# An attention and mixture-of-experts kernel on one core: exponentials and last sums in PSUM, scaling on ScalarE, kept blocks on SP's queue, shared PSUM banks

## The chip, the cores and the metric

The kernel runs on one core of a Trainium2 chip. The metric is the device time of one execution in microseconds: the median of several runs, and beside it one profiled execution, from which all views come. The engines are TensorE (PE in the profile; PEld is its weight load), VectorE (DVE), ScalarE (ACT), GpSimd (POOL) and SyncE (SP, which only issues transfers). PSUM, which TensorE writes, has eight banks of 512 fp32 values per partition.

## The reference

Attention over 4 batches, 8 heads, 768 positions and 64 channels, with a local window of 96 positions, 8 global positions and a linear distance bias for each head; then four experts of two products each, weighted by `domain_probs`.

```python
scores = scale * q @ k^T + bias            # masked to the window and the global positions
a = exp(scores - max); a = a / (a.sum(-1) + 1e-9)
x = (a @ v) as [3072, 512]
p = domain_probs / (domain_probs.sum(-1) + 1e-9)
for e in range(4):
    out += p[:, e:e+1] * (relu(x @ w1[e]) @ w2[e])
```

## The kernel before

Every matrix of the large products is split into two fp32r parts, a rounded one and the rest, and each product is three matmuls. The attention of batch 0 runs alone at the start (`early=True`, plain fp32 operands); the attention of batch b+1 then runs beside the experts of batch b; the last batch's experts run alone.

**Attention.** Heads go in pairs, a pair has six tiles of 128 positions. `flow` (line 472) is one step of a software pipeline of four stages: the scores of a new tile, the softmax of the tiles of the two steps before, the transposition (`turn`, line 434) of the next older one, and, once three tiles are collected, the products with v (`weigh`, line 446). In `softmax` (line 402), for each of the two heads, VectorE adds the bias to the scores, writes `pb` in SBUF and takes the row's extreme; ScalarE takes the exponential in `pb` and sums it into `zsum`; for the older tile VectorE adds 1e-9, takes the reciprocal and multiplies `pb`. The score tile `ps` holds both heads, 256 columns each. `prepare` (line 493) makes the operands of a pair in six steps: transposes through PSUM tiles `pt`, the split of q into `st_q` and of k into `kd`, and four transfers that copy a half of `st_q` to `qd`, of which there is one buffer. `prepare_early` (line 356) does it for the start; there VectorE writes the second half of the partitions of `early_q` and ScalarE the first, both from one `pt`.

**Experts.** A unit is a quarter of one expert's hidden columns: sixteen units a batch. `first` (line 730) makes the hidden part h by seven block products in place of eight (a Strassen scheme), each of six matmuls with 384 columns into a PSUM tile `pm`. VectorE adds each `pm` to earlier sums in SBUF (`p1`, `u`, `vv`, `c22`); ScalarE's ReLU makes the rounded part of h; the rest of h is put on the list `late` and made by VectorE after the next addition. `second` (line 769) makes six groups of six matmuls with 512 columns, and VectorE adds each to `acc`. `blocks` (line 587) makes the seven operand blocks (`xB`, `xT`) from the next batch's x, on VectorE, ScalarE and GpSimd, during the last products of a batch.

**Weights.** In batch 0 `load_w1` and `load_w2` (lines 648 and 688) load and split each unit's weights on ScalarE and GpSimd, step by step beside the products, and `keep` (line 639) writes the split block to DRAM by GpSimd's queue at once. Later batches fetch it by SP's queue, which also carries q, k, v, the raw weights and the copies to `qd`.

**PSUM banks.** At the start: three `ps`, four `pt`, one `px`. Later: three `pm`, two `ps`, two `pt`, one `px`.

**Order.** To the seventh step of batch 0's experts each engine's instructions stay in program order (`Ordered.on`). After that a list scheduler orders them, with program order as its priority, and tracks dependences and buffers.

Of the kernel before, what the change touches and what calls it, by code (L numbers as in the profile page):

```python
# [9 lines left out]
F32 = mybir.dt.float32  # L10
# [8 lines left out]
P = 128  # L19
# [6 lines left out]
def f32(ap):  # L26
    return ap.bitcast(F32)
# [158 lines left out]
def attn_moe_kernel(ctx: ExitStack, tc, q, k, v, n_global, n_local, domain_probs, w1, w2, out):  # L186
# [88 lines left out]
    class Pools:  # L275


        def __init__(self, stack, name, st, kd, qd, nat, natv, pb, ps, pt):
            def sbuf(part, bufs):
                return stack.enter_context(tc.tile_pool(name=f"{name}_{part}", bufs=bufs))  # L280

            def psum(part, bufs):
                return stack.enter_context(tc.tile_pool(name=f"{name}_{part}", bufs=bufs, space=PSUM))

            self.st, self.natv = sbuf("st", st), sbuf("natv", natv)
            self.kd, self.qd, self.nat, self.vg = sbuf("kd", kd), sbuf("qd", qd), sbuf("nat", nat), sbuf("vg", kd)
            self.pb, self.pT, self.small = sbuf("pb", pb), sbuf("pT", 4), sbuf("small", pb)
            self.ps, self.pt, self.px = psum("ps", ps), psum("pt", pt), psum("px", 1)
# [33 lines left out]

    def prepare_q(A, nat, hf, got):

        tp = transpose_half(A, nat, hf)
        st = A.st.tile([P, 2, HALF], F32R, name="st_q")
        ac.activation(st[:, 0, :], tp[:, :HALF], AF.Copy, scale=-SCALE)
        yield
        ve.scalar_tensor_tensor(
            st[:, 1, :], tp[:, :HALF], -SCALE, f32(st[:, 0, :]), op0=ALU.mult, op1=ALU.subtract  # L330
        )
        qd = got[("q", hf)] = A.qd.tile([P, 2, 2, HALF], F32R, name="qd")
        for j in range(2):
            for n in range(2):
                sy.dma_start(f32(qd[n * D : (n + 1) * D, j]), f32(st[j * D : (j + 1) * D]))

    def prepare_k(A, nat, hf, got):
# [11 lines left out]
        yield  # L349
# [52 lines left out]
    def softmax(A, new, old):  # L402
# [12 lines left out]
        for j in range(2):  # L415
            if new:
                ve.tensor_tensor_reduce(
                    new["pb"][:, j, pcol], ps[:, j, cols], nbias[:, 2 * pr + j, bcol],
                    1.0, 3.0e38, ALU.add, ALU.min, nmax[:, j : j + 1],
                )  # L420
                ac.activation(
                    new["pb"][:, j, pcol], new["pb"][:, j, pcol], AF.Exp, bias=nmax[:, j : j + 1], scale=-1.0,
                    accum_out=new["zsum"][:, j : j + 1],
                )
            if old:
                if j == 0:
                    ve.tensor_scalar_add(zsum, zsum, 1e-9)
                else:
                    ve.reciprocal(zsum, zsum)
        if old:  # L430
            for j in range(2):
                ve.tensor_scalar_mul(pb[:, j, old["pcol"]], pb[:, j, old["pcol"]], zsum[:, j : j + 1])
# [13 lines left out]
    def weigh(A, three, x):  # L446

        px = A.px.tile([P, 512], F32, name="px")
# [17 lines left out]
    def attention(b, A, early=False):  # L466
# [5 lines left out]
        def flow(new=None):  # L472

            one, two, three, four = tiles
            if new:
                new["ps"] = scores(A, new["t"], gots[new["pr"]], early)
            if three and not early:
                turn(A, three)
            softmax(A, one, two)
            if three and early:  # L480
                turn(A, three)
            if four:
                turned.append(four)
                if len(turned) == TPH:
                    weigh(A, turned, x)
                    turned.clear()
            tiles[:] = [new, one, two, three]
# [5 lines left out]
        def prepare(nat, got):  # L493

            got["v"] = nat
            q0, q1 = (prepare_q(A, nat["q"], hf, got) for hf in range(2))
            k0, k1 = (prepare_k(A, nat["k"], hf, got) for hf in range(2))
            next(q0)
            yield 1
            next(q0, None)  # L500
            next(k0)
            yield 1
            next(k0, None)
            yield 1
            next(k1)
            yield 1
            nat["vg"] = windows(A, nat["v"])
            next(k1, None)
            next(q1)
            yield 1  # L510
            next(q1, None)
# [125 lines left out]
    kept = {}  # L637

    def keep(key, dst):
        kept[key] = dp.tile(list(dst.shape), F32R, name="kept_{}_{}_{}".format(*key))  # L640
        po.dma_start(f32(kept[key]), f32(dst))
# [6 lines left out]
    def load_w1(i, wait=0, lead=5, hold=2):  # L648
# [37 lines left out]
        keep((e, g, 1), dst)  # L686

    def load_w2(i, lead=7):
# [17 lines left out]
        keep((e, g, 2), dst)  # L706
# [23 lines left out]
    def first(i):  # L730
# [13 lines left out]
        p1, u, vv, c22 = (up.tile([P, HALF], F32, name=n) for n in ("p1", "u", "vv", "c22"))  # L744
# [8 lines left out]
        add(c22, pm, vv)  # L753
        add(u, pm, u)
        relu(1, 1, c22)
        yield
        add(p1, product(i, "A12", "B21"), p1)
        relu(0, 0, p1)
        yield
        add(vv, product(i, "S4", "B22"), vv)  # L760
        relu(0, 1, vv)
        yield
        add(u, product(i, "A22", "T4"), u)
        relu(1, 0, u)
# [4 lines left out]
    def second(i):  # L769

        b, e, g = units[i]
        w2s, h = wts[(i, 2)], hs[i]
# [32 lines left out]
    with ExitStack() as start_stack:  # L805
        A = Pools(start_stack, "start", st=1, kd=2, qd=1, nat=2, natv=3, pb=4, ps=3, pt=4)
# [14 lines left out]
    ps_mm = main.enter_context(tc.tile_pool(name="ps_mm", bufs=3, space=PSUM))  # L821
    A = Pools(main, "att", st=1, kd=1, qd=1, nat=1, natv=1, pb=2, ps=2, pt=2)
# [79 lines left out]
```

## Time and profile before

| | us |
|---|---|
| median of 3 runs | 1236.85 (1235.83 to 1238.42) |
| the profiled execution | 1238.11 |
| its span | 1236.3 |
| mean granted TensorE clock | 0.989 |

The span runs from the first to the last instruction. Stages: attention alone to about 80 us; experts of batch 0 with the attention of batch 1 to about 380; two more such batches to about 675 and 970; the last batch alone to 1230. A wait is put down to what ended last before the waiting instruction began. The busy time of an engine leaves out waits; of overlapping matmuls the union is counted.

### The profile page before, as it was taken

What the parts mean: (1) busy time and instruction counts of PE and PEld (TensorE: products, weight loads), DVE (VectorE), ACT (ScalarE), POOL (GpSimd) and SP (SyncE); (2) the same over time, 40 slices, a digit from 0 to 9 for tenths busy, and PEclk for the clock granted to TensorE, in tenths of its full rate; (3) what the DMA queues carried; (4) which work ended last, traced back from release to release, by engine and by line L of the source; (5) the groups of instructions that cost most, each with busy time, mean ns of one, the idle gap of its engine ahead of it and who ended that gap; (6) DMA issues with size and microseconds to landing.
All of it is one profiled execution on the core that took longest, in us unless ns stands there. A gap on an engine that the chain in (4) does not pass through costs nothing.

```text
span 1236.3 us, 18009 instructions
## 1 busy us (share of the span) xinstructions
PE 1184.1 (96%) x6624; PEld 1055.6 (85%) x6624; DVE 922.9 (75%) x2018; ACT 429.7 (35%) x1044; POOL 241.2 (20%) x258
## 2 busy tenths in 40 slices
PE   6779999999999999999999999999999999999998
PEld 4558898888888898898987898899898899999996
DVE  6878989877868777777767776867776866666665
ACT  4764454545442333333323233333332211111110
POOL 5576657466541000000002000000000100000000
PEclk9989999999999999999999999999999999999999
DMA  6557868786856666576655765757554555555532
GB/s 160 156 158 249 286 212 278 239 282 230 295 183 210 228 197 207 189 228 194 222 169 176 263 195 193 232 166 248 191 170 179 181 213 187 188 187 187 187 128 88
DMA packets 122704, 251.39 MB, mean 203 GB/s; under 512 B 83184, under 2 KB 91376, under 8 KB 106224
## 3 DMA queue, kind: packets, MB, share of 16 engines
q1 hardware_dynamic: 114256, 197.73, 50.5%
q0 software_dynamic: 4608, 46.14, 9.2%
q10 hardware_dynamic: 3744, 6.30, 1.4%
q8 instruction: 54, 0.88, 0.3%
q14 instruction: 42, 0.34, 0.1%
HBM read 174.11 MB, written 52.43 MB: 183 GB/s over the span
## 4 chain that ended last, share of the span: by engine, by line
PE 81%; DVE 9%; DMA 5%; ACT 2%; issue 1%; SPq 1%; POOL 1%; ACTq 0%; DVEq 0%; POOLq 0%
PE pm L42 71%; DMA qd<-st_q 5%; PE pt L42 4%; PE px L42 3%; PE ps L42 3%; DVE pb L42 3%; DVE h L42 1%; SPq L42 1%; DVE x L42 1%; ACT pb L42 1%; DVE zsum L42 1%; DVE u L42 1%; DVE xT L42 0%; DVE acc L42 0%; DVE vv L42 0%
## 5 line engine op out<-in xcount | busy, mean ns | idle before, releaser
L42 PE MATMUL pm<-w2s,h 128*128 128x512 f32 x2304 | 558.5, 396 | 9.5 <-DVE acc L42 9.1
L42 PEld LDWEIGHTS pm<-w2s,h 128*128 128x128 f32 x2304 | 429.1, 189 | 101.3 <-DVE acc L42 12.3
L42 DVE SCALAR_TENSOR_TENSOR acc<-pm,prob,acc 128x512 f32<-128x512 f32 x360 | 267.4, 748 | 120.9 <-PE pm L42 119.1
L42 PE MATMUL pm<-xT,w1s 128*128 128x384 f32 x1536 | 298.4, 339 | 4.9 <-ACT xT L42 3.0
L42 PEld LDWEIGHTS pm<-xT,w1s 128*128 128x128 f32 x1536 | 268.3, 189 | 8.2 <-ACT xT L42 3.4
L42 PE MATMUL pm<-xB,w1s 128*128 128x384 f32 x1152 | 229.1, 340 | 2.2 <-DVE vv L42 1.3
L42 PEld LDWEIGHTS pm<-xB,w1s 128*128 128x128 f32 x1152 | 202.5, 189 | 8.1 <-DVE vv L42 1.6
L42 ACT ACTIVATE pb<-pb,nmax 128x256 f32<-128x256 f32 (+1 forms) x192 | 93.1, 486 | 121.3 <-DVE nmax L42 114.2
L42 POOL COPY vg<-v 32x768 f32<-32x768 f32 x16 | 13.3, 829 | 525.7 <-DMA v<-in_v_dram 515.2
L42 ACT COPY p<-pm 128x384 f32<-128x384 f32 x64 | 30.6, 477 | 214.0 <-PE pm L42 213.9
L42 DVE TENSOR_SCALAR pb<-pb,zsum 128x256 f32<-128x256 f32 (+1 forms) x192 | 84.9, 474 | 2.8
L42 DVE TENSOR_TENSOR u<-pm,p 128x384 f32<-128x384 f32 x64 | 35.6, 556 | 61.1 <-PE pm L42 57.5
L42 DVE CUSTOM_DVE_ANT_0 pb<-ps,nbias 128x256 f32<-128x256 f32 (+1 forms) x192 | 71.9, 395 | 10.9 <-PE ps L42 7.1
L42 ACT ACTIVATE h<-c 128x384 fp32r<-128x384 f32 x64 | 33.6, 525 | 131.8 <-DVE c L42 131.8
L42 ACT COPY pT<-pt 128x512 f32<-128x512 f32 (+1 forms) x96 | 52.2, 544 | 76.0 <-PE pt L42 75.7
L42 DVE TENSOR_TENSOR u<-pm,u 128x384 f32<-128x384 f32 x128 | 70.5, 551 | 3.3 <-PE pm L42 2.6
L42 PE MATMUL pt<-ident,pb 128*128 128x128 f32 x352 | 57.2, 280 | 13.6 <-DVE pb L42 13.0
L42 PEld LDWEIGHTS pt<-ident,pb 128*128 128x128 f32 x352 | 43.3, 143 | 22.6 <-DVE pb L42 6.3
L42 PE MATMUL ps<-kd,qd 128*128 128x256 f32 x288 | 48.6, 283 | 6.0 <-DMA qd<-st_q 6.0
L42 PEld LDWEIGHTS ps<-kd,qd 128*128 128x128 f32 x288 | 44.5, 188 | 11.2 <-issue 7.2
L42 DVE TENSOR_TENSOR c<-pm,vv 128x384 f32<-128x384 f32 x64 | 35.6, 556 | 22.4 <-PE pm L42 21.7
L42 DVE TENSOR_TENSOR vv<-pm,u 128x384 f32<-128x384 f32 x64 | 35.6, 556 | 21.7 <-PE pm L42 21.0
(89 smaller groups left out, 1117.6 us busy)
## 6 DMA issues: line engine op xcount, KB each, us to landing
w1s<-kept SPq DMA_DIRECT2D x48, 1792.0 KB, 7.4
w2s<-kept SPq DMA_DIRECT2D x48, 1024.0 KB, 5.0
kept<-w1s POOLq DMA_DIRECT2D x16, 1792.0 KB, 6.6
qd<-st_q SPq DMA_DIRECT2D x96, 192.0 KB, 6.2
raw<-in_moe_w_dram SPq DMA_DIRECT2D x32, 512.0 KB, 4.4
kept<-w2s POOLq DMA_DIRECT2D x16, 1024.0 KB, 6.6
v<-in_v_dram SPq DMA_DIRECT2D x16, 384.0 KB, 4.2
out_dram<-acc ACTq DMA_DIRECT2D x24, 256.0 KB, 3.0
```

The source lines that it names most:

```text
L42: ins = fn(*args, **kwargs)
```

## The change

- At the start (`A.early`) the biased scores and the exponentials are written over the scores in `ps`; VectorE scales from there into `pb`. `ps` gets four banks, `pt` three.
- In the other batches the exponentials stay in `pb`, and both the addition of 1e-9 and the scaling move to ScalarE.
- `px` has no bank of its own there: it takes a buffer of `pt`. `pm` gets four banks.
- `weigh` comes before the transposition and the softmax in a step.
- The last four sums of `first` are written over `pm`; ReLU and the rest read `pm`. The tile `c22` goes.
- `prepare` makes q's and k's halves whole, in the order q0, k0, q1, k1.
- The kept blocks are written by SP's queue, when the unit's `first` or `second` begins.

```diff
-            self.ps, self.pt, self.px = psum("ps", ps), psum("pt", pt), psum("px", 1)
+            self.ps, self.pt = psum("ps", ps), psum("pt", pt)
+            self.px, self.pxname = (psum("px", px), "px") if px else (self.pt, "pt")
...
+                e = new.setdefault("exp", {})[j] = ps[:, j, cols] if A.early else new["pb"][:, j, pcol]
                 ve.tensor_tensor_reduce(
-                    new["pb"][:, j, pcol], ps[:, j, cols], nbias[:, 2 * pr + j, bcol],
-                    1.0, 3.0e38, ALU.add, ALU.min, nmax[:, j : j + 1],
+                    e, ps[:, j, cols], nbias[:, 2 * pr + j, bcol], 1.0, 3.0e38, ALU.add, ALU.min, nmax[:, j : j + 1]
                 )
                 ac.activation(
-                    new["pb"][:, j, pcol], new["pb"][:, j, pcol], AF.Exp, bias=nmax[:, j : j + 1], scale=-1.0,
-                    accum_out=new["zsum"][:, j : j + 1],
+                    e, e, AF.Exp, bias=nmax[:, j : j + 1], scale=-1.0, accum_out=new["zsum"][:, j : j + 1]
                 )
             if old:
-                if j == 0:
+                if j == 1:
+                    ve.reciprocal(zsum, zsum)
+                elif A.early:
                     ve.tensor_scalar_add(zsum, zsum, 1e-9)
                 else:
-                    ve.reciprocal(zsum, zsum)
+                    ac.activation(zsum, zsum, AF.Copy, bias=1e-9)
         if old:
             for j in range(2):
-                ve.tensor_scalar_mul(pb[:, j, old["pcol"]], pb[:, j, old["pcol"]], zsum[:, j : j + 1])
+                if A.early:
+                    ve.tensor_scalar_mul(pb[:, j, old["pcol"]], old["exp"][j], zsum[:, j : j + 1])
+                else:
+                    ac.activation(pb[:, j, old["pcol"]], old["exp"][j], AF.Copy, scale=zsum[:, j : j + 1])
...
                 new["ps"] = scores(A, new["t"], gots[new["pr"]], early)
+            if four:
+                turned.append(four)
+                if len(turned) == TPH:
+                    weigh(A, turned, x)
+                    turned.clear()
             if three and not early:
                 turn(A, three)
             softmax(A, one, two)
             if three and early:
                 turn(A, three)
-            if four:
-                turned.append(four)
-                if len(turned) == TPH:
-                    weigh(A, turned, x)
-                    turned.clear()
...
-            q0, q1 = (prepare_q(A, nat["q"], hf, got) for hf in range(2))
-            k0, k1 = (prepare_k(A, nat["k"], hf, got) for hf in range(2))
-            next(q0)
-            yield 1
-            next(q0, None)
-            next(k0)
...
+            prepare_q(A, nat["q"], 0, got)
+            yield 1
+            prepare_k(A, nat["k"], 0, got)
+            yield 1
+            prepare_q(A, nat["q"], 1, got)
+            yield 1
+            prepare_k(A, nat["k"], 1, got)
             yield 1
             nat["vg"] = windows(A, nat["v"])
-            next(k1, None)
-            next(q1)
-            yield 1
-            next(q1, None)
+            yield 1
             yield 1
...
-    def keep(key, dst):
-        kept[key] = dp.tile(list(dst.shape), F32R, name="kept_{}_{}_{}".format(*key))
-        po.dma_start(f32(kept[key]), f32(dst))
+    def keep(i, n):
+
+        if (i, n) in waiting:
+            key, dst = waiting.pop((i, n))
+            kept[key] = dp.tile(list(dst.shape), F32R, name="kept_{}_{}_{}".format(*key))
+            sy.dma_start(f32(kept[key]), f32(dst))
...
-        keep((e, g, 1), dst)
+        waiting[(i, 1)] = (e, g, 1), dst
...
+        def last(pm, other):
+
+            add(pm[:, :HALF], pm, other)
+            return pm[:, :HALF]
+
+        p1, u, vv = (up.tile([P, HALF], F32, name=n) for n in ("p1", "u", "vv"))
+        keep(i, 1)
...
         pm = product(i, "S3", "T3")
-        add(c22, pm, vv)
         add(u, pm, u)
-        relu(1, 1, c22)
-        yield
-        add(p1, product(i, "A12", "B21"), p1)
-        relu(0, 0, p1)
-        yield
-        add(vv, product(i, "S4", "B22"), vv)
-        relu(0, 1, vv)
-        yield
-        add(u, product(i, "A22", "T4"), u)
-        relu(1, 0, u)
+        relu(1, 1, last(pm, vv))
+        yield
+        relu(0, 0, last(product(i, "A12", "B21"), p1))
+        yield
+        relu(0, 1, last(product(i, "S4", "B22"), vv))
+        yield
+        relu(1, 0, last(product(i, "A22", "T4"), u))
...
+        keep(i, 2)
         w2s, h = wts[(i, 2)], hs[i]
...
-        A = Pools(start_stack, "start", st=1, kd=2, qd=1, nat=2, natv=3, pb=4, ps=3, pt=4)
+        A = Pools(start_stack, "start", st=1, kd=2, qd=1, nat=2, natv=3, pb=4, ps=4, pt=3, px=1, early=True)
...
-    ps_mm = main.enter_context(tc.tile_pool(name="ps_mm", bufs=3, space=PSUM))
-    A = Pools(main, "att", st=1, kd=1, qd=1, nat=1, natv=1, pb=2, ps=2, pt=2)
+    ps_mm = main.enter_context(tc.tile_pool(name="ps_mm", bufs=4, space=PSUM))
+    A = Pools(main, "att", st=1, kd=1, qd=1, nat=1, natv=1, pb=2, ps=2, pt=2, px=0, early=False)
```

More of the change, by code (lines that the diff above doesn't have):

```diff
@@ L275, in attn_moe_kernel, with __init__ @@
     class Pools:
-        def __init__(self, stack, name, st, kd, qd, nat, natv, pb, ps, pt):
+        def __init__(self, stack, name, st, kd, qd, nat, natv, pb, ps, pt, px, early):
+            self.early = early
             def sbuf(part, bufs):
@@ L446, in weigh @@
     def weigh(A, three, x):
-        px = A.px.tile([P, 512], F32, name="px")
+        px = A.px.tile([P, 512], F32, name=A.pxname)
         for i, tile_ in enumerate(three):
@@ L495, in prepare @@
             got["v"] = nat
-            q0, q1 = (prepare_q(A, nat["q"], hf, got) for hf in range(2))
-            k0, k1 = (prepare_k(A, nat["k"], hf, got) for hf in range(2))
-            next(q0)
+            prepare_q(A, nat["q"], 0, got)
             yield 1
-            next(q0, None)
-            next(k0)
+            prepare_k(A, nat["k"], 0, got)
             yield 1
-            next(k0, None)
+            prepare_q(A, nat["q"], 1, got)
             yield 1
-            next(k1)
+            prepare_k(A, nat["k"], 1, got)
             yield 1
             nat["vg"] = windows(A, nat["v"])
-            next(k1, None)
-            next(q1)
             yield 1
-            next(q1, None)
             yield 1
@@ L636, in attn_moe_kernel @@
     dp = main.enter_context(tc.tile_pool(name="dp", bufs=1, space=bass.MemoryType.DRAM))
-    kept = {}
-    def keep(key, dst):
-        kept[key] = dp.tile(list(dst.shape), F32R, name="kept_{}_{}_{}".format(*key))
-        po.dma_start(f32(kept[key]), f32(dst))
+    kept, waiting = {}, {}
+    def keep(i, n):
[3 more added lines that the diff above has]
+            sy.dma_start(f32(kept[key]), f32(dst))
     def fetch(name, key, shape, view):
@@ L705, in load_w2 @@
             yield 1
-        keep((e, g, 2), dst)
+        waiting[(i, 2)] = (e, g, 2), dst
     hs = {}
@@ L742, in add @@
             work_late()
-        p1, u, vv, c22 = (up.tile([P, HALF], F32, name=n) for n in ("p1", "u", "vv", "c22"))
+        def last(pm, other):
[3 more added lines that the diff above has]
+        keep(i, 1)
         pm = product(i, "A11", "B11")
```

## The prediction

> **What bounds the kernel now.** I read the page's totals first, then the waits of TensorE, then the chain of waits, and after that each stage by itself.
>
> ```profile
> PE 1184.1 (96%) x6624; PEld 1055.6 (85%) x6624; DVE 922.9 (75%) x2018; ACT 429.7 (35%) x1044; POOL 241.2 (20%) x258
> ```
>
> TensorE is busy for 96%, but its matmuls overlap, so this figure hides short stops. The pace is read better from the chain of waits (start, length, what): groups that run without a stop near the end of the third batch, then the last batch, which has no attention beside it.
>
> ```profile
> 940.70 3.13 PE pm L42 x18
> 944.26 5.48 PE pm L42 x24
> 967.97 262.21 PE pm L42 x1302
> ```
>
> A 384-column matmul takes 3.13/18 = 0.174 us, a 512-column one 5.48/24 = 0.228. A batch has 672 and 576 of them: 117 + 131 = 248 us. The last batch runs at that pace, so the diff can win only where TensorE stops. The waits (total, times, longest), first of the whole run, then of 100 to 340 us, then of 660 to 680:
>
> ```profile
> PE pt L42 <- DVE pb L42: 13.0, 16, 1.9
> PE pm L42 <- DVE acc L42: 9.1, 6, 2.0
> PE ps L42 <- DMA qd<-st_q: 6.0, 8, 2.0
> ...
> PE pm L42 <- DVE acc L42: 3.1, 3, 1.3
> PE pm L42 <- DVE vv L42: 1.3, 1, 1.3
> PE pm L42 <- DVE u L42: 0.8, 1, 0.8
> PE pm L42 <- DVE p L42: 0.3, 1, 0.3
> ...
> PE pm L42 <- DVE acc L42: 2.0, 1, 2.0
> ```
>
> There are three places to change: the start, where attention runs alone (its wait is for pb); VectorE's lags in the first mixed batch (3.1 + 1.3 + 0.8 + 0.3 = 5.5 us); and the three batch boundaries, 2.0 us each. The windows show what else a boundary costs, and what the start is bound by (columns: PE, PEld, DVE, ACT, POOL busy, granted clock, DMA share, GB/s):
>
> ```profile
> 11.30:76.60 65.30, 50.36 (x368) 39.53 (x368) 57.13 (x214) 46.70 (x146) 33.26 (x36) 0.96 0.48 138
> ...
> 378.70:382.10 3.40, 3.37 (x8) 2.70 (x9) 2.56 (x4) 0.83 (x1) 0.00 (x0) 0.50 0.02 8
> 675.60:679.00 3.40, 3.40 (x10) 2.62 (x9) 3.40 (x5) 1.66 (x2) 0.00 (x0) 0.50 0.00 0
> 969.20:972.50 3.30, 3.30 (x9) 2.55 (x8) 3.29 (x5) 1.62 (x2) 0.00 (x0) 0.50 0.00 0
> ```
>
> After each boundary's stop the granted clock is 0.50 for 3.4 us, which costs 1.7 us more: 3 x (2.0 + 1.7) = 11.1 us in all. In the start VectorE is busy 57.1 of 65.3 us, and its only long wait there is 6.3 us for `early_q`: the start is VectorE's.
>
> **The change, part by part.**
>
> *Start: exponentials in PSUM.* The groups of VectorE between 11.3 and 76.6 us (24 tiles):
>
> ```profile
> L42 DVE TENSOR_SCALAR pb<-pb,zsum 128x256 f32<-128x256 f32 x39 | 18.9, 526 | 0.7
> L42 DVE CUSTOM_DVE_ANT_0 pb<-ps,nbias 128x256 f32<-128x256 f32 x40 | 16.6, 415 | 0.1
> L42 DVE TENSOR_SCALAR zsum<-zsum 128x2 f32<-128x2 f32 x24 | 6.5, 271 | 0.0
> L42 DVE TENSOR_SCALAR pb<-pb,zsum 128x128 f32<-128x128 f32 x8 | 4.6, 610 | 0.1
> ...
> L42 DVE COPY early_k<-pt 128x384 f32<-128x384 f32 x7 | 3.9, 551 | 0.7 <-PE pt L42 0.7
> ...
> L42 DVE CUSTOM_DVE_ANT_0 pb<-ps,nbias 128x128 f32<-128x128 f32 x8 | 2.2, 285 | 1.4 <-PE ps L42 1.4
> ```
>
> The scaling reads and writes SBUF and is stretched, to 610 ns for half the columns; the add that reads PSUM is not (415 and 285 ns). From PSUM I give the scaling those prices: 39 x (526 - 415) + 8 x (610 - 285) = 6.9 us less. What VectorE pays to write PSUM, no row shows; I take zero more, and for the range the 0.11 us by which the two prices above differ, 48 x 0.11 = 5.3 us to either side.
>
> Against this stands a wait that the diff does not name. Both heads' exponentials now lie in one tile `ps`, 2 x 256 x 4 bytes, one bank. The timeline shows how the program treats a bank that two engines use (start, length, engine):
>
> ```profile
> 41.49 0.48 ACT L42 ACTIVATE early_q<-pt 64x384 f32<-64x384 f32 x1
> 42.01 0.56 DVE L42 TENSOR_SCALAR early_q<-pt 64x384 f32<-64x384 f32 x1 [1.39 <-ACT early_q L42]
> 42.82 0.08 DVE L42 DVE_READ_ACCUMULATOR2_ANT nmax<- 128x1 f32 x1
> 43.00 0.40 ACT L42 ACTIVATE pb<-pb,nmax 128x128 f32<-128x128 f32 x1 [0.26 <-DVE nmax L42]
> 46.20 0.51 ACT L42 ACTIVATE pb<-pb,nmax 128x256 f32<-128x256 f32 x1 [0.74 <-DVE zsum L42]
> 46.61 0.18 ACT L42 ACTIVATION_READ_ACCUMULATOR pb<-pb,nmax 128x1 f32 x1
> ```
>
> The two halves of `early_q` share nothing but the bank of `pt` that they read, on different partitions, yet VectorE starts 0.04 us after ScalarE ends. So the second head's add will wait for the first head's exponential. The hop to ScalarE is 0.10 us (42.90 to 43.00), exponential and accumulator 0.59 (46.20 to 46.79), the hop back 0.04: 0.73 us, in which VectorE, in program order, has only the sum of `zsum` (0.27) to do. It idles 0.46 x 24 = 11.0 us.
>
> The Trainium skill, "PSUM — Partial Sum Buffer", section "PSUM bank collisions raise a hardware error", says that two engines may be in one bank at once only in different quadrants of 32 partitions. By it the halves of `early_q` could have run together, which this trace contradicts with its 0.04 us; for exponentials on all 128 partitions rule and row both give the wait, and the sum by the rule alone is the same.
>
> ScalarE's queue adds to the wait, since a first exponential now holds VectorE up wherever ScalarE is late.
>
> ```profile
> L42 ACT COPY pT<-pt 128x512 f32<-128x512 f32 x80 | 46.4, 580 | 76.0 <-PE pt L42 75.7
> L42 ACT CAST w1s<-sums 128x512 fp32r<-128x512 f32 x32 | 18.6, 615 | 1.3 <-POOL sums L42 1.3
> L42 ACT COPY x<-px 128x384 f32<-128x384 f32 x32 | 15.3, 479 | 39.8 <-PE px L42 39.7
> ```
>
> Between the end of a tile's second exponential and the next first one VectorE leaves ScalarE about 0.8 us (two scalings 0.83, next add 0.42, a hop 0.10, less the 0.59 of the exponential). The copy to `pT` (0.58) fits; with a weight cast (0.615) behind it, ScalarE is 0.4 us late, less where VectorE copies keys: 12 casts x 0.3 = 3.5 us. Start: 11.0 - 6.9 + 3.5 = **+7.6 us** (+2 to +13).
>
> *Products: four banks, last sums in place.* One boundary, in the timeline:
>
> ```profile
> 371.49 0.79 DVE L42 SCALAR_TENSOR_TENSOR h<-c,h 128x384 fp32r<-128x384 f32 x1
> 372.67 1.87 DVE L42 SCALAR_TENSOR_TENSOR h<-p,h 128x384 fp32r<-128x384 f32 x1
> 374.93 2.14 DVE L42 TENSOR_TENSOR xT<-x,xT 128x768 fp32r<-128x768 f32 x1
> 377.94 2.06 DVE L42 SCALAR_TENSOR_TENSOR acc<-pm,prob,acc 128x512 f32<-128x512 f32 x3
> 378.73 3.64 PE L42 MATMUL pm<-w2s,h 128*128 128x512 f32 x8 [2.01 <-DVE acc L42]
> ```
>
> TensorE has filled its three banks and waits for the first `acc`, behind stretched work with two SBUF inputs. With its source in PSUM I price `h<-p` at 0.55 (the key copy above, 551 ns, reads PSUM at that width): 1.3 us earlier. A fourth bank gives TensorE six more matmuls, 6 x 0.228 = 1.4 us. Together this exceeds the stop of 2.0 us; but four of the seven sums now keep their bank through ReLU (about the 0.48 of the x copy) and the rest (0.55), so I leave 0.5 us a boundary, without the half clock: 3 x (3.7 - 0.5) = **-9.6 us** (0 to -11.1). The same bank and the lighter VectorE should take 4.5 of the 5.5 us of lags in the first mixed batch: **-4.5** (0 to -5.5). For the other batches nothing is left to win.
>
> *Scaling on ScalarE in the mixed batches.* The rows of 97 to 357 us:
>
> ```profile
> L42 DVE TENSOR_SCALAR pb<-pb,zsum 128x256 f32<-128x256 f32 x40 | 28.2, 731 | 0.5
> L42 DVE TENSOR_SCALAR zsum<-zsum 128x2 f32<-128x2 f32 x24 | 10.7, 444 | 2.7 <-ACT pb L42 2.7
> ```
>
> VectorE loses about 39 us of work in that batch, ScalarE gains 48 x 0.5 + 24 x 0.2 = 29 us. ScalarE is busy 35% overall, so this lies beside TensorE's work, and its gain is already in the lags above. What it can cost is a ReLU or a `pT` copy behind a scaling (0.5 us), now that ReLU holds a bank. The products with v lose their own bank: 8 a batch wait at worst for one `pT` copy (0.58), 14 us in three batches; no transposition waits for its bank now, so I take **+1** for both.
>
> *Kept blocks on SP's queue, and the preparation's order.* The DMA issues (KB each, us to landing):
>
> ```profile
> kept<-w1s POOLq DMA_DIRECT2D x16, 1792.0 KB, 6.6
> qd<-st_q SPq DMA_DIRECT2D x96, 192.0 KB, 6.2
> ```
>
> GpSimd is spared 32 issues, on no path. On SP, 32 big writes (w2's too) now stand among the loads and the `qd` copies in the first mixed batch; SP waits there only for splits that the products need anyway. The second half of q is prepared earlier, but `qd` has one buffer, so its copies still cannot leave before the scores of tile 2: the 6.0 us of waits for `qd` stay. The copies of 4 second halves have no slack; with a w1 or w2 block ahead 8 times in 10, by half of 6.6 us, 4 x 0.8 x 3.3 = 10.6 us is the upper end, zero the lower. Total traffic is unchanged, and a copy ahead of a block gains, so I take **+2.5**.
>
> Sum: 7.6 - 9.6 - 4.5 + 1 + 2.5 = -3.0 us. The profiled execution took 1238.1 us (span 1236.3, 1.8 around it), 1.3 over the median, so 1235.1 there and 1233.9 against the median: **1234 us**.
>
> **The rivals.**
>
> 1. *Slower, by the start.* The diff puts the products with v, and their copy `x`, ahead of the exponentials in program order. Every third tile the first exponential then waits for 24 matmuls (the chain has 1.46 us for 24) and a copy of 0.48; less 0.4 us of slack that is 1.5 x 8 = 12 us more, 1246. It decides as soon as the start loses 10.6 us instead of 7.6. Against it: TensorE is idle for 15 of the 65 us and may be done early.
> 2. *The fourth bank is eaten up.* If ReLU and rest hold the banks as long as the fourth one lasts, the boundaries still stop for 2.0 us and drop to half clock: 1243.5. For it: ReLU shares ScalarE with the casts of the next batch's blocks there; against it: VectorE is 1.3 us earlier in any case.
> 3. *The add does not wait for the exponential.* Then the start wins 6.9 us, less 2 for a ScalarE that becomes nearly as full: 1233.9 - 7.6 - 4.9 = 1221.5. Against it stands the `early_q` row.
> 4. *Copies of q behind the kept blocks.* With the upper end of 10.6 us, 1242. The Trainium skill, "DMA: Bandwidth & Descriptors", section "Queues, rings and completion order", says that a DMA engine alternates between queue rows packet by packet but takes one row's ring in order; by that rule the move makes this rival likelier. No run here shows it yet.
>
> **How the numbers follow.** Forecast 55%, its own range 1229 to 1239; rivals 12, 10, 15 and 8%. A difference under 0.2% (2.5 us) cannot be told from no change here. Of the forecast's 55, some 32 lie below 1234.4, 15 within 2.5 us of 1236.85 and 8 above; with rival 3 faster has 47%, with rivals 1, 2 and 4 slower has 38%, and 15% is left for the same. The range 1222 to 1245 takes in most of rivals 2 and 4, half of 3 and part of 1.
>
> **What would show it.** The start: the first product begins some 7 us later, and VectorE's waits between 11 and 85 us list a new one for ScalarE's `ps`, about 0.5 us x 24, while its scaling takes about 415 ns. Boundaries: no wait of 2.0 us for `acc`, and a clock of 1.00 after them. Mixed batches: TensorE's waits for `acc`, `vv`, `u` and `p` under 1 us in all. If the wait for `ps` is missing, rival 3 holds; if the windows at the boundaries still show 0.50, rival 2; if TensorE's wait for `qd` passes 10 us, rival 4. A last batch longer than 262 us would mean that the banks do not suffice even without attention, which I have not priced.

## The result and the profile after

| | before | after |
|---|---|---|
| median of 4 runs, us | 1236.34 (1234.34 to 1238.42) | 1221.84 (1221.52 to 1223.60) |
| ratio | 1 | 0.9885 (95%: 0.9869 to 0.9901) |
| span of the profiled execution, us | 1236.3 | 1221.8 |
| mean granted clock | 0.989 | 0.994 |

The kernel is 1.15% faster: 14.2 us at the time of before. The forecast was 1234, which is 0.24% less than before. By the ratio the prediction's before of 1236.85 would become 1222.6 us: at the lowest edge of the range of 1222 to 1245, and below the 1229 to 1239 that the forecast had as its own. So the sign was right and the size was not.

The page's totals of the changed kernel, to be set against the same line of before:

```profile
PE 1176.3 (96%) x6624; PEld 1049.2 (86%) x6624; DVE 835.0 (68%) x1802; ACT 492.9 (40%) x1260; POOL 213.2 (17%) x226
```

VectorE lost 88 us of work, 922.9 to 835.0, and ScalarE gained 63. The waits of TensorE over the whole run (total, times, longest):

```profile
PE pm L42 <- DVE h L42: 3.2, 5, 1.1
...
PE ps L42 <- DMA qd<-st_q: 1.9, 3, 1.1
```

The 9.1 us for `acc` are gone, and of the 6.0 us for `qd` 1.9 are left. Four stretches make up the difference; they are read from one profiled execution of each kernel.

**The start is longer.** The first large product, in the timeline of before (start, length, engine, operation):

```profile
79.83 0.79 PE L42 MATMUL pm<-xB,w1s 128*128 128x384 f32 x3
```

and in the changed kernel:

```profile
92.26 0.79 PE L42 MATMUL pm<-xB,w1s 128*128 128x384 f32 x3
```

It begins 12.4 us later. VectorE's waits from 11.3 to 89.0 us of the changed kernel show why:

```profile
DVE ps L42 <- ACT ps L42: 17.7, 21, 1.9
```

VectorE now waits 17.7 us for ScalarE's exponentials in `ps`. One tile in the timeline:

```profile
44.97 0.45 ACT L42 ACTIVATE ps<-ps,nmax 128x256 f32<-128x256 f32 x1 [1.18 <-DVE nmax L42]
45.34 0.19 ACT L42 ACTIVATION_READ_ACCUMULATOR ps<-ps,nmax 128x1 f32 x1
45.56 0.43 DVE L42 CUSTOM_DVE_ANT_0 ps<-ps,nbias 128x256 f32<-128x256 f32 x1 [0.55 <-ACT ps L42]
```

The second head's add (45.56) starts 0.03 us after ScalarE has read its accumulator for the first head (45.34 + 0.19), although the two heads use different columns: they share the bank.

**The handoff is shorter.** The handoff is the stretch behind the first product, in which the operand blocks are finished beside the products. Here are its large products, in windows of TensorE with the tile `pm` alone (length, busy, matmuls, granted clock, DMA share, GB/s), before:

```profile
79.83:96.93 17.10, 12.40 (x43) 0.70 0.96 303
79.83:119.83 40.00, 31.78 (x132) 0.87 0.78 263
```

and after:

```profile
92.26:109.36 17.10, 15.80 (x78) 1.00 0.95 322
92.26:132.26 40.00, 35.35 (x168) 1.00 0.80 265
```

Before, 43 matmuls in 17.1 us at a clock of 0.70; after, 78 at 1.00. In 40 us the changed kernel is 36 matmuls ahead; at its pace of 40/168 = 0.24 us, 8.6 of the 12.4 us are won back. About 5 of these are the clock: before was granted 0.50 in the window from 85.2 to 95.2 us, behind its first product, the changed kernel in that from 84.7 to 91.4, ahead of it. What sets these stretches is not shown. No step of the forecast holds this.

**The boundaries don't stop.** Where before stood still for 2.0 us and then ran at half clock, the windows after show (PE, PEld, DVE, ACT, POOL, clock):

```profile
373.80:382.00 8.20, 8.20 (x38) 6.68 (x37) 8.20 (x11) 1.98 (x3) 1.43 (x1) 1.00 0.46 188
662.00:670.00 8.00, 8.00 (x36) 6.28 (x35) 8.00 (x9) 1.69 (x3) 1.66 (x1) 1.00 0.49 203
952.00:960.00 8.00, 8.00 (x37) 6.61 (x36) 7.65 (x12) 2.22 (x4) 2.28 (x2) 1.00 0.59 220
```

The chain of waits ends in one piece now, which begins in the last group ahead of the boundary:

```profile
951.21 264.67 PE pm L42 x1320
```

Three boundaries at 3.7 us are 11.1 us. Of these, 3 x 1.7 = 5.1 us are the half clock, and it does not follow from the stops alone: kept_only below stops for 2.0 us at the same three boundaries and keeps a clock of 1.00.

**The mixed batches and the last one.** The last batch keeps its pace: 262.21/1302 and 264.67/1320 are both 0.201 us a matmul. 12.4 - 8.6 - 11.1 = -7.3 us; the other 6.9 us must lie inside the mixed batches. From 100 to 340 us TensorE's waits are now

```profile
PE pm L42 <- DVE h L42: 2.5, 3, 1.1
```

where before had 5.5 us for `acc`, `vv`, `u` and `p`. Part of both lies in the 40 us that are counted above (before 1.3 us for `vv` and 1.3 for `acc`, after 1.1 for h), so 2.8 us against 1.4 are left here. The wait for `qd` is 4.1 us shorter in the whole run. That makes 1.4 + 4.1 = 5.5 of the 6.9 us; where the other 1.4 come from is not shown.

### The profile page after: what moved, and what is told of

It is laid out like the page before. It is cut to its first block, busy times and chain, and to the rows that moved or that the text cites. A ratio compares the mean times of both kernels' runs of the same rounds, so it can differ in the third digit from the quotient of the medians.

```text
span 1221.8 us, 18005 instructions
## 1 busy us (share of the span) xinstructions
PE 1176.3 (96%) x6624; PEld 1049.2 (86%) x6624; DVE 835.0 (68%) x1802; ACT 492.9 (40%) x1260; POOL 213.2 (17%) x226
## 4 chain that ended last, share of the span: by engine, by line
PE 83%; DMA 5%; ACT 4%; DVE 4%; POOL 2%; issue 2%; SPq 0%; ACTq 0%; POOLq 0%; DVEq 0%
PE pm L42 74%; PE pt L42 6%; PE ps L42 3%; DMA qd<-st_q 3%; DMA raw<-in_moe_w_dram 2%; ACT ps L42 2%; DVE ps L42 1%; POOL sums L42 1%; ACT pT L42 1%; POOL w2s L42 1%; POOL w1s L42 1%; SPq L42 0%; PE px L42 0%; DVE pb L42 0%; DVE early_q L42 0%
## 5 line engine op out<-in xcount | busy, mean ns | idle before, releaser
L42 PE MATMUL pm<-w2s,h 128*128 128x512 f32 x2304 | 551.5, 393 | 3.2 <-DVE h L42 3.2
L42 ACT ACTIVATE h<-pm 128x384 fp32r<-128x384 f32 x256 | 124.7, 491 | 177.1 <-DVE pm L42 173.8
L42 DVE SCALAR_TENSOR_TENSOR h<-pm,h 128x384 fp32r<-128x384 f32 x256 | 140.7, 552 | 12.3 <-ACT h L42 8.6
L42 ACT ACTIVATE pb<-pb,nmax 128x256 f32<-128x256 f32 (+1 forms) x144 | 69.9, 487 | 90.4 <-DVE nmax L42 89.8
L42 DVE TENSOR_TENSOR pm<-pm,vv 128x384 f32<-128x384 f32 x128 | 71.6, 560 | 1.4 <-PE pm L42 1.3
L42 ACT ACTIVATE pb<-pb,zsum 128x256 f32<-128x256 f32 (+1 forms) x144 | 63.2, 485 | 18.6 <-DVE zsum L42 18.6
L42 DVE CUSTOM_DVE_ANT_0 pb<-ps,nbias 128x256 f32<-128x256 f32 (+1 forms) x144 | 52.6, 396 | 7.5 <-PE ps L42 3.9
L42 DVE TENSOR_TENSOR u<-pm,u 128x384 f32<-128x384 f32 x64 | 35.6, 557 | 24.1 <-PE pm L42 23.1
L42 POOL TENSOR_TENSOR w2s<-raw,w2s 128x512 fp32r<-128x512 f32 x32 | 40.9, 1293 | 56.2 <-ACT w2s L42 56.2
```

The source lines that it names most:

```text
L42: ins = fn(*args, **kwargs)
```

## The experiments

The kernel before took 1236.0, 1233.7 and 1233.0 us beside the three groups of runs below, so ratios are compared, each to before on its own chip; 0.001 is 1.24 us. The changed kernel stands at 0.9885. It was not run again beside these groups, and the kernel before moved by 3 us between them, so a small difference to the changed kernel has a doubtful size: dve_scale and sums_sbuf are 6.4 and 7.2 us above it by the ratios, 3.8 and 4.1 by the times as they stand. An edit also lets the scheduler order everything behind it anew, and part of a difference may come from that.

| run | us | ratio (95%) |
|---|---|---|
| start_sbuf | 1213.16 | 0.9825 (0.9797 to 0.9852) |
| weigh_late | 1219.23 | 0.9878 (0.9850 to 0.9907) |
| head1_psum | 1206.61 | 0.9775 (0.9748 to 0.9803) |
| kept_pool | 1229.18 | 0.9948 (0.9928 to 0.9968) |
| three_banks | 1247.97 | 1.0122 (1.0105 to 1.0138) |
| sums_sbuf | 1225.95 | 0.9943 (0.9926 to 0.9960) |
| dve_scale | 1225.59 | 0.9937 (0.9921 to 0.9954) |
| head1_weigh_late | 1210.56 | 0.9821 (0.9805 to 0.9837) |
| banks_only | 1221.84 | 0.9925 (0.9897 to 0.9952) |
| kept_only | 1235.40 | 1.0019 (1.0004 to 1.0033) |
| kept_sp_now | 1237.77 | 1.0042 (1.0023 to 1.0060) |
| q_dve_first | 1202.17 | 0.9749 (0.9725 to 0.9773) |

### The start

**start_sbuf**: the changed kernel with the exponentials of the start in SBUF again.

```diff
-e = new.setdefault("exp", {})[j] = ps[:, j, cols] if A.early else new["pb"][:, j, pcol]
+e = new.setdefault("exp", {})[j] = new["pb"][:, j, pcol]
```

> The changed kernel, but at the start the biased scores and exponentials lie in pb (SBUF) as before; banks, order of weigh and all else as changed. In the changed kernel the first product begins at 92.3 us, before at 79.8. Theory (the second head's add waits for the first head's exponential, because both lie in one bank): VectorE's wait for ScalarE's ps (13.9 us) goes, the scaling is stretched again to some 530 ns, and the first product begins at 78 to 83 us; the total falls by most of that, to about 1211 us (1208 to 1216). Rival (weigh's copy x ahead of the exponentials is what lengthens the start): the first product stays past 88 us and the total within 4 us of 1221.8.

Its first large product in the timeline:

```profile
78.84 0.79 PE L42 MATMUL pm<-xB,w1s 128*128 128x384 f32 x3
```

VectorE's scaling in its start (groups from 11.3 to 76.6 us: busy, mean ns, idle before):

```profile
L42 DVE TENSOR_SCALAR pb<-pb,zsum 128x256 f32<-128x256 f32 x40 | 19.3, 523 | 0.7
```

and in the changed kernel:

```profile
L42 DVE TENSOR_SCALAR pb<-ps,zsum 128x256 f32<-128x256 f32 x30 | 13.1, 480 | 0.6
...
L42 DVE TENSOR_SCALAR pb<-ps,zsum 128x128 f32<-128x128 f32 x8 | 2.4, 346 | 0.2
```

As the theory of the bank wait said: the wait for `ps` is gone, the scaling is stretched again, and the start is 13.4 us shorter than in the changed kernel. The total gains 0.60%, 7.4 us: the 13.4 us at the start don't reach the end whole. Part is lost soon behind it: from 100 to 181 us TensorE waits 6.8 us (3.8 for h, 1.8 for `st_q`, 1.2 for `pb`), in the changed kernel from 100 to 195 us 3.4 (2.5 for h, 0.9 for `st_q`).

**weigh_late**: at the start the products with v and the copy `x` stand last in the step again, as in the kernel before.

```diff
-            if four:
+            if four and not early:
...
             if three and early:
                 turn(A, three)
+            if four and early:
+                turned.append(four)
...
```

> The changed kernel, but at the start weigh comes after softmax and turn, as before. Theory (bank wait): every tile still loses its half microsecond, the first product begins no more than 4 us earlier than 92.3, total 1218 to 1222. Rival (order of weigh): eight tiles no longer wait for the copy x, 1.3 us each, the first product begins at about 82 us and the total falls to about 1211.

The first large product:

```profile
88.74 0.79 PE L42 MATMUL pm<-xB,w1s 128*128 128x384 f32 x3
```

VectorE's wait from 11.3 to 85.4 us:

```profile
DVE ps L42 <- ACT ps L42: 12.4, 21, 0.7
```

3.5 us earlier, the longest wait 0.7 in place of 1.9: copies of `x` ahead of an exponential do hold VectorE up, by about what the theory said. In the total this can't be told from nothing (0.9878 beside 0.9885). The bank alone then makes the start 8.9 us longer (88.74 - 79.83).

**head1_psum**: the first head's exponential in SBUF, only the second head's in PSUM.

```diff
-e = new.setdefault("exp", {})[j] = ps[:, j, cols] if A.early else new["pb"][:, j, pcol]
+e = new.setdefault("exp", {})[j] = ps[:, j, cols] if A.early and j == 1 else new["pb"][:, j, pcol]
```

> The changed kernel, but at the start only the second head's scores and exponentials stay in PSUM, the first head's go to pb. Theory (bank wait): the second add no longer waits for the first exponential, and half of the scalings are free of stretching, so the first product begins earlier than in either kernel, at 76 to 81 us, and the total is 1207 to 1214. Rival (any exponential in PSUM, or the order of weigh, lengthens the start): the first product begins at 86 us or later, total 1216 to 1222.

The first large product:

```profile
76.75 0.80 PE L42 MATMUL pm<-xB,w1s 128*128 128x384 f32 x3
```

Scalings and exponentials of the two heads (groups from 11.3 to 76.6 us):

```profile
L42 DVE TENSOR_SCALAR pb<-pb,zsum 128x256 f32<-128x256 f32 x20 | 11.5, 576 | 0.8
L42 ACT ACTIVATE pb<-pb,nmax 128x256 f32<-128x256 f32 x20 | 10.2, 510 | 8.2 <-DVE nmax L42 4.9 <-DVE zsum L42 3.3
L42 DVE TENSOR_SCALAR pb<-ps,zsum 128x256 f32<-128x256 f32 x20 | 9.5, 473 | 0.0
L42 ACT ACTIVATE ps<-ps,nmax 128x256 f32<-128x256 f32 x20 | 8.7, 437 | 0.6 <-DVE zsum L42 0.6
```

VectorE's longest wait of that stretch:

```profile
DVE early_q L42 <- ACT early_q L42: 5.2, 7, 1.3
```

Half of the scalings are spared the stretch, and no add meets an exponential in its bank, since the second head's add comes ahead of its own exponential only. The product begins within the 76 to 81 of the theory, the total just below its range, and at 0.9775 it beats both kernels. The wait for `early_q` is now VectorE's longest there.

**q_dve_first**: head1_psum, with VectorE writing its half of `early_q` ahead of ScalarE's.

```diff
-            ac.activation(zq[:D, 0, pl, :], tpv[:D], AF.Copy, scale=-SCALE)
...
+            ac.activation(zq[:D, 0, pl, :], tpv[:D], AF.Copy, scale=-SCALE)
```

> The changed kernel with only the second head's exponential in PSUM at the start (1206.6 us, first large product at 76.8), and with VectorE writing its half of the first blocks of q ahead of ScalarE's half instead of behind it, both from one bank. Theory (a bank that two engines use is taken in program order, whatever the partitions; the wait of 5 us in 7 times falls on whoever comes second, and ScalarE has the time): VectorE's wait for ScalarE's early_q goes, the first large product begins 2 to 5 us earlier (72 to 75), total 1202 to 1205. Rival (ScalarE, now second, is late for the transposes and exponentials): first product within 1 us of 76.8 and total 1205.5 to 1208.

The first large product:

```profile
72.14 0.80 PE L42 MATMUL pm<-xB,w1s 128*128 128x384 f32 x3
```

The wait for `early_q`, now ScalarE's, from 11.3 to 76.6 us:

```profile
ACT early_q L42 <- DVE early_q L42: 2.2, 5, 0.6
```

As the theory said, one swapped line moves the wait from the engine that sets the start to the other one, and the products begin 4.6 us earlier. This is the fastest version, 31 us under the kernel before (0.9749).

**head1_weigh_late**: head1_psum and weigh_late together.

```diff
+... ps[:, j, cols] if A.early and j == 1 else new["pb"][:, j, pcol]
...
+            if four and not early:
...
+            if four and early:
...
```

> At the start only the second head's exponentials in PSUM and weigh after turn, the rest as in the changed kernel. Theory (the order of weigh costs about 3 us wherever it stands, as with both heads in PSUM): 1202 to 1205. Rival (without the wait for the bank ScalarE has slack, and the order of weigh costs nothing): 1205.5 to 1208, as with weigh first.

The first product begins at 76.66, as in head1_psum: without the wait for the bank the order of weigh costs the start nothing, as the rival said. But the total is 4 us above head1_psum, a miss for theory and rival. Between 105 and 180 us it does 294 large products where head1_psum does 307. TensorE's waits from 100 to 180 us are 6.9 us there (3.8 for h, 1.8 for `st_q`, 1.3 for `pb`) and 3.2 in head1_psum (2.3 for h, 0.9 for `st_q`), which is about the 4 us. These orders are the scheduler's; why this one makes VectorE and ScalarE later stays open.

### The products

**banks_only**: the kernel before with four banks for `pm` and none for `px`, nothing else.

```diff
...
-    ps_mm = main.enter_context(tc.tile_pool(name="ps_mm", bufs=3, space=PSUM))
-    A = Pools(main, "att", st=1, kd=1, qd=1, nat=1, natv=1, pb=2, ps=2, pt=2)
+    ps_mm = main.enter_context(tc.tile_pool(name="ps_mm", bufs=4, space=PSUM))
+    A = Pools(main, "att", st=1, kd=1, qd=1, nat=1, natv=1, pb=2, ps=2, pt=2, px=0)
```

> The kernel before with one edit: large products get four banks, and the products with v take theirs from the pool of the transposes. Theory (the stops at the boundaries come from the want of a bank while acc is late, and 24 more matmul of 0.228 us per bank cover most of it): each boundary's wait for acc falls from 2.0 us to under 0.8 us, no window of granted clock 0.50 stands behind a boundary, and the lags of the first mixed batch fall by half; total 8 to 13 us below the kernel before (1223 to 1228). Rival (the lighter VectorE and the sums left in the bank are what removes the stops; the bank alone is used up): waits for acc of 1.3 us or more and windows of 0.50 stay, total within 5 us of the kernel before.

The three boundaries, TensorE's rows in the timeline with the stop in brackets:

```profile
372.83 3.51 PE L42 MATMUL pm<-w2s,h 128*128 128x512 f32 x14 [1.25 <-DVE acc L42]
...
663.42 3.92 PE L42 MATMUL pm<-w2s,h 128*128 128x512 f32 x16 [0.98 <-DVE acc L42]
...
953.59 3.69 PE L42 MATMUL pm<-w2s,h 128*128 128x512 f32 x15 [0.99 <-DVE acc L42]
```

The stops are 1.0 to 1.25 us, not the under 0.8 expected, but the windows around them (366 to 376, 657 to 667, 947 to 957) show a clock of 1.00. (A bank holds one group of six matmuls, 6 x 0.228 = 1.4 us, and not the 24 of the expectation.) The bank shortens each stop by about 2.0 - 1.1 = 0.9 us; against the profile of before, with its half clock, it wins (2.0 + 1.7) - 1.1 = 2.6 us a boundary. That the shorter stop is what kept the clock up is not shown, since kept_only kept it with stops of 2.0 us. In the first mixed batch the waits for `acc`, `u` and `p` are gone and `vv` is down to 0.3. Total -0.75% (-0.48 to -1.03), 9.3 us.

**sums_sbuf**: the changed kernel with the four last sums in SBUF, `c22` back.

```diff
...
+            out = other if out is None else out
-            add(pm[:, :HALF], pm, other)
-            return pm[:, :HALF]
+            add(out, pm, other)
+            return out
...
-        relu(1, 1, last(pm, vv))
+        relu(1, 1, last(pm, vv, c22))
```

> The changed kernel with four banks, but the last four sums go to SBUF as before (c22 is back), ReLU and rest read SBUF. Theory (the gain in the mixed batches comes from the fourth bank and the scaling moved off VectorE): boundaries keep a clock of 1.00, total 1219 to 1225. Rival (the gain comes from sources in PSUM, whose rest GpSimd cannot stretch): the rest rises from 552 ns to 580 or more, boundaries stop again, total 1228 or more.

The costliest group of the rest of h, over the whole run, here:

```profile
L42 DVE SCALAR_TENSOR_TENSOR h<-p,h 128x384 fp32r<-128x384 f32 x64 | 42.8, 669 | 0.6 <-ACT h L42 0.5
```

and in the changed kernel:

```profile
L42 DVE SCALAR_TENSOR_TENSOR h<-pm,h 128x384 fp32r<-128x384 f32 x256 | 140.7, 552 | 12.3 <-ACT h L42 8.6
...
L42 DVE TENSOR_TENSOR pm<-pm,vv 128x384 f32<-128x384 f32 x128 | 71.6, 560 | 1.4 <-PE pm L42 1.3
L42 DVE TENSOR_TENSOR vv<-pm,u 128x384 f32<-128x384 f32 x64 | 35.7, 557 | 26.9 <-PE pm L42 25.9
```

and at its second boundary, in TensorE's timeline of sums_sbuf:

```profile
667.30 7.10 PE L42 MATMUL pm<-w2s,h 128*128 128x512 f32 x30 [0.50 <-DVE u L42]
675.00 5.28 PE L42 MATMUL pm<-w2s,h 128*128 128x512 f32 x22 [0.60 <-DVE acc L42]
```

From PSUM the rest takes 552 ns on the mean of the run, and a sum written into PSUM 560 as against 557 into SBUF. With the sums in SBUF the boundary stops again, 1.1 us in two pieces, with the clock at 1.00 in the window from 667 to 677; the total rises by 0.58%, a little over the theory's upper end. Both signs of the rival are there, the longer rest and the stops, but not its total and no half clock. The sums in place and the bank each do part of the boundary.

**three_banks**: the changed kernel with the old banks, three `pm` and one `px`.

```diff
-... bufs=4 ... px=0, early=False)
+... bufs=3 ... px=1, early=False)
```

> The changed kernel, but the products have three banks again and the products with v their own one. Theory (the fourth bank pays for the boundaries, and sums left in PSUM need it): the boundaries stop again for about 2 us with a granted clock of 0.5 after them, and since four sums a unit hold their bank through ReLU and rest, even the last batch, alone, takes longer than its 248 us; total 1235 or more. Rival (the lighter VectorE alone removes the stops): total within 4 us of 1221.8, last batch 248 us.

TensorE's longest wait in the whole run:

```profile
PE pm L42 <- DVE h L42: 11.8, 26, 1.3
```

The window from 1000 to 1200 us, where no attention runs beside the experts, with `pm` alone:

```profile
1000.00:1200.00 200.00, 198.15 (x977) 1.00 0.51 183
```

and in the changed kernel:

```profile
1000.00:1200.00 200.00, 200.00 (x1009) 1.00 0.49 177
```

TensorE does 977 large products in 200 us where the changed kernel does 1009, and so does the kernel before, with three banks and its sums in SBUF. Sums that stay in their bank keep it for ReLU and rest; without the fourth bank they cost more than they win, 1.2% over the kernel before. The half clock at the boundaries, which the theory expected too, didn't come.

**dve_scale**: in the mixed batches 1e-9 and scaling on VectorE again.

```diff
-                    ac.activation(zsum, zsum, AF.Copy, bias=1e-9)
+                    ve.tensor_scalar_add(zsum, zsum, 1e-9)
...
-                    ac.activation(pb[:, j, old["pcol"]], old["exp"][j], AF.Copy, scale=zsum[:, j : j + 1])
+                    ve.tensor_scalar_mul(pb[:, j, old["pcol"]], old["exp"][j], zsum[:, j : j + 1])
```

> The changed kernel, but in the mixed batches zsum and the scaling stay on VectorE. Theory (VectorE's lags in the first mixed batch, stretched by GpSimd, are relieved by the move): the first mixed batch loses 3 to 5 us, the two others less than 2, total 1225 to 1229. Rival (four banks hide VectorE's lags, and the move to ScalarE is worth nothing): total within 2.5 us of 1221.8.

The group in the first mixed batch (97 to 357 us):

```profile
L42 DVE TENSOR_SCALAR pb<-pb,zsum 128x256 f32<-128x256 f32 x40 | 26.1, 677 | 0.6
```

677 ns on VectorE, stretched, where ScalarE takes 503 in the changed kernel. Total 0.52% slower (3.8 us by the times), as the theory said; the scaling's move is a gain of its own, also beside four banks.

### The kept blocks

**kept_pool**: the changed kernel with the kept blocks written by GpSimd's queue at once.

```diff
+    def keep_now(key, dst):
+        kept[key] = dp.tile(list(dst.shape), F32R, name="kept_{}_{}_{}".format(*key))
+        po.dma_start(f32(kept[key]), f32(dst))
...
-        waiting[(i, 1)] = (e, g, 1), dst
+        keep_now((e, g, 1), dst)
```

> The changed kernel, but the split weights are written to DRAM by GpSimd's queue as soon as they are split, as before. From the first product to the 42nd the changed kernel takes 10.8 us, the kernel before 17.1. Theory (on SP the kept blocks hold back the raw loads, so that GpSimd has no sums to make while VectorE makes the operand blocks): the raw loads come early again, VectorE's subtraction x is stretched to over 3 us again, and the stretch grows back to 15 to 17 us, total 1226 to 1229. Rival (the shorter stretch comes from the four banks and the lighter VectorE): it stays at 11 to 12 us and the total within 3 us of 1221.8.

Its window behind the first product:

```profile
92.55:109.65 17.10, 13.92 (x60) 0.90 0.91 288
```

GpSimd in its timeline:

```profile
94.09 1.03 POOL L42 TENSOR_TENSOR xB<-x,xB 128x384 fp32r<-128x384 f32 x1
95.06 1.76 POOL L42 TENSOR_TENSOR sums<-raw 128x256 f32<-128x256 f32 x2
...
101.58 1.30 POOL L42 TENSOR_TENSOR xT<-x,xT 128x384 fp32r<-128x384 f32 x1
```

GpSimd in the changed kernel:

```profile
93.77 1.03 POOL L42 TENSOR_TENSOR xB<-x,xB 128x384 fp32r<-128x384 f32 x1 [0.93 <-ACT xB L42]
97.86 1.01 POOL L42 TENSOR_TENSOR xT<-x,xT 128x384 fp32r<-128x384 f32 x1 [3.06 <-ACT xT L42]
```

With the writes on GpSimd the sums and splits of the next weights stand between the block rests (the parts that GpSimd makes of `xB` and `xT`), and the rest in `xT` comes 7.5 us after `xB` instead of 4.1. Why GpSimd has these sums to do here shows in SP's issues of the raw weights, in this run:

```profile
60.68 29.48 SPq L42 DMA_DIRECT2D raw<-in_moe_w_dram  x2
```

and in the changed kernel:

```profile
93.72 2.29 SPq L42 DMA_DIRECT2D raw<-in_moe_w_dram  x2
```

Here both are issued by 60.68 + 29.48 = 90.16 us, ahead of the first product at 92.55. In the changed kernel they come behind two kept writes that SP issues at 92.86, as the theory said: SP's queue holds the raw loads back, and GpSimd has no sums to make yet. The theory's other sign, VectorE's subtraction `x` of over 3 us, did not return: its second one took 1.30 us here, 1.25 in the changed kernel and 3.43 in before. 60 large products in 17.1 us in place of 78: the handoff loses less than the theory said, the total a little more than its 1226 to 1229. Moving the writes to SP is worth 0.63% here, 7.8 us by the medians; the profiled executions are 3.8 us apart.

**kept_only**: that move alone, in the kernel before.

```diff
-        po.dma_start(f32(kept[key]), f32(dst))
+            sy.dma_start(f32(kept[key]), f32(dst))
...
-        keep((e, g, 1), dst)
+        waiting[(i, 1)] = (e, g, 1), dst
...
+        keep(i, 1)
...
```

> The kernel before with one edit: the kept blocks of weights are written by SP's queue at the start of their products instead of by GpSimd's at once. Theory (what won 7.3 us in the changed kernel is that GpSimd takes the rest of x's first blocks ahead of the next weights' sums, so that the first mixed batch has no stretched VectorE work in it): the first 42 large products take 3 us less or better than in the kernel before (14 us or less against 17.1), total 4 to 8 us below it (1228 to 1232). Rival (the gain needs the other edits, four banks above all): within 3 us of the kernel before.

Its window behind the first product:

```profile
80.19:97.29 17.10, 15.39 (x78) 1.00 0.94 320
```

TensorE's waits of its whole run:

```profile
PE pm L42 <- DVE acc L42: 10.9, 9, 2.0
```

TensorE behind its second boundary's stop, in the timeline and as a window:

```profile
673.28 7.09 PE L42 MATMUL pm<-w2s,h 128*128 128x512 f32 x30 [1.99 <-DVE acc L42]
...
673.28:681.00 7.72, 7.72 (x34) 1.00 0.30 92
```

The handoff is won, as the theory said: 78 matmuls at full clock. But the total is 0.19% above before, as the rival said and a little worse. What was won is lost again behind the handoff, where VectorE is late: for `acc` 9 times (10.9 us; before 6 times, 9.1), and for `u` once by 2.8 us, before by 0.8 at most, with a clock of 0.50 behind it (window 239.7 to 246.5). The three boundaries still stop, for 2.01, 1.99 and 1.99 us, and yet the clock behind each stays at 1.00, where the profile of before has 0.50. That four banks and a lighter VectorE take such waits up, as in the changed kernel, fits its rows; four banks and this move alone were not run together.

**kept_sp_now**: the changed kernel, SP's queue, but at once behind the split.

```diff
+    def keep_now(key, dst):
...
+        sy.dma_start(f32(kept[key]), f32(dst))
...
-        waiting[(i, 1)] = (e, g, 1), dst
+        keep_now((e, g, 1), dst)
...
```

> The changed kernel, with the kept blocks on SP's queue as there, but issued at once behind their split, as the kernel before did on GpSimd's. Theory (the engine that issues them decides, since GpSimd is then free and its work comes in the better order): 1220 to 1225. Rival (the time of issue decides: an issue that waits for the split holds up the loads behind it on SP, and GpSimd's order falls back): 1227 to 1231, with SP idle in front of the kept writes, and first 42 products of 13.5 us or more.

SP's longest waits from 92 to 400 us:

```profile
SPq L42 <- POOL w1s L42: 96.7, 15, 25.8
```

The timeline at one of them, GpSimd's split and SP's issues:

```profile
293.62 2.53 POOL L42 TENSOR_TENSOR w1s<-sums,w1s 128x512 fp32r<-128x512 f32 x2
...
296.17 0.34 SPq L42 DMA_DIRECT2D kept<-w1s  x1
```

SP's issue before these is at 288.98; it then stands at `kept<-w1s` until GpSimd's split ends (293.62 + 2.53 = 296.15), and its next `qd` copies, at 298.93, come behind that. In the changed kernel these waits for `w1s` are 43.7 us (8 times). Handoff as in the changed kernel (76 products in 17.1 us), but from 243 to 355 us TensorE waits 3.8 us for a `qd` copy and 5.1 for h, and the total is 0.42% above before. So both matter: which engine issues, for the handoff; when it issues, for the rest. The theory's 1220 to 1225 fell, and the loss was larger than the rival's.

## Why the prediction was right in sign and wrong in size

- **What bounds the kernel**: right. All gains but the handoff's came from the three places named, and the last batch didn't change.
- **Start, +7.6**: measured +12.4 at the first product; with the order of before +8.9 (weigh_late). The bank wait was foreseen and is there: 12.4 us in 21 waits with weigh late, for 11.0 + 3.5. The scaling was mis-sized: it fell from 523 and 611 ns to 480 and 346, (43 x 40 + 265 x 8)/1000 = 3.8 us and not 6.9. Rival 1's mechanism, copies of `x` ahead of exponentials, added 3.5 us and 5.3 us of wait (17.7 - 12.4), a third of what it was priced at, and nothing where the first head's exponential stands in SBUF (head1_weigh_late, 76.66 beside 76.75).
- **Fourth bank and last sums, -9.6, and lags, -4.5**: right against the profile of before. The boundaries run at full clock without a stop, 11.1 us, of which the 5.1 us of half clock were taken as the price of a stop; kept_only's stops did not pay it. The bank alone gives 9.3 us with its share of the lags (banks_only), and undoing the sums costs 0.58% (4.1 us by the times). The wait for h in their place is 3.2 us in all.
- **Scaling and shared bank, +1**: wrong sign. "Its gain is already in the lags above" didn't hold: without it the changed kernel is 0.52% slower by the ratios. The cover by ScalarE held: in the mixed batches TensorE lists no wait for `px` behind a `pT` copy. The changed kernel's 7.2 us of such waits, 7 times, all lie in the start, where `px` keeps its own bank and the products with v stand earlier.
- **Kept blocks, +2.5**: this is the step that failed most. It priced what the writes do on SP, and alone that is the price (kept_only, +2.4 us, 0.5 to 4.1). It counted GpSimd's side as "32 issues, on no path", and there the move changed the order: the raw loads came later, the block rests came ahead of sums and splits, and in the changed kernel the move is worth 0.63% in the other direction. It also let the 6.0 us of waits for `qd` stay; they are 1.9 us in the changed kernel, 1.9 with the move alone (kept_only) and 2.5 without it (kept_pool). The step is off by 2.5 + 7.8 = 10.3 us; the forecast as a whole was 11.3 too high (14.2 - 2.9), the start having been too low by 4.8 and, by the ratios, the scaling too high by 1 + 6.4. Such single steps needn't add up to the whole, since each was undone beside the others.
- **Rivals**: 2 and 4 fell: no half clock, and the wait for `qd` went down to 1.9 us though `kept<-w1s` takes longer to land. 3 fell with the wait of 17.7 us; that its time of 1221.5 came out is chance. By the queue rule of "DMA: Bandwidth & Descriptors" (the Trainium skill, "Queues, rings and completion order") rival 4 was to be likelier; kept_sp_now shows such a loss, 3.8 us for one `qd` copy, behind an SP that stands still at its issue; no run here tells a delay in the ring apart from that.
- **The bank rule**: by the Trainium skill, "PSUM — Partial Sum Buffer", section "PSUM bank collisions raise a hardware error", the halves of `early_q`, on different partitions, could run together. They take turns in whichever order they are written (q_dve_first: 2.2 us of wait on ScalarE in place of 5.2 on VectorE). That is the program's waiting, and so the 0.04 us did not contradict the page, as the prediction has it; what the chip would allow was not tried.

## What to carry to other kernels

A PSUM tile that two engines use by turns costs a hop for each turn, even in different columns or partitions (each such tile here fills one bank, so the runs don't tell tile and bank apart): put what one engine changes while the other goes on in another bank, and let the less busy engine be the one that comes second. When an instruction leaves an engine, look at what that engine does next and not only at where the instruction goes. Parts of a change are not worth the same alone: four banks pay alone, sums that hold their bank pay only with them, and the kept blocks' move pays only in company.

## What was not expected of the hardware

- ScalarE's exponential of 256 columns took 437 ns in PSUM and 510 in SBUF, in one kernel (head1_psum).
- VectorE's scaling took 473 to 480 ns at the start from PSUM, and from SBUF 523 to 576 there and 677 beside GpSimd's work in the first mixed batch (dve_scale). The Trainium skill, "SBUF — State Buffer", section "Who interferes with whom", says that a VectorE instruction with at most one SBUF input, outside its two-port modes, isn't held up by GpSimd. The 552 ns of `h<-pm,h` (one of its two inputs in PSUM), beside 669 of `h<-p,h`, agree; in the last batch, from 1000 to 1200 us, where GpSimd has nothing to do, `h<-p,h` took 548 (sums_sbuf).
- TensorE's stops of 2.0 us at the three boundaries were followed by 3.4 us of a granted clock of 0.50 in before and by 1.00 in kept_only; stops of 1.0 to 1.25 us there left it at 1.00 (banks_only). The length of a stop alone did not decide.
